# A gated state-space and linear-attention kernel: from a hand-written issue order to a list scheduler at trace time

## The chip, the cores and the metric

The kernel runs on one core of a Trainium2 chip. The metric is the device time of one execution in microseconds (us). Times are medians over all executions of a run. An execution is marked "slow" when it is over 1.5% above the fastest of the same kernel; ratios leave such executions out. A profile is one execution, so its span can differ by a microsecond or two from the median.

Engine names: PE is TensorE (matmuls; PEld is its weight load), DVE is VectorE, ACT is ScalarE, POOL is GpSimd, SP is SyncE, which issues the DMAs. The engines run side by side; in this program each takes its own instructions in the order in which they were issued, and waits on semaphores for the others. SBUF is the memory that the engines work in, PSUM the one into which PE writes its results; copying a result from PSUM to SBUF is called its evacuation. A fold multiplies a weight matrix with another one once, before the work on the rows. The tail is the time from PE's last matmul to the end.

## The reference, cut to what matters

The input is a sequence x of 2048 rows and 512 columns. Two branches are computed from it and mixed row by row by a sigmoid gate.

```python
x = A_x                                              # (1, 2048, 512)
g = _sigmoid((x * gate_w).sum(-1, keepdims=True))
# branch a: a diagonal complex recurrence over the rows
Bu = jnp.einsum("bld,pd->blp", x + 0j, B_bar)
for t in range(L):
    h = Lam_bar[None, :] * h + Bu[:, t, :]
y = 2.0 * jnp.einsum("blp,dp->bld", hseq, Cmat).real + x * Dskip
# branch b: linear attention, 32 heads of 16, softmax features of both signs
phi_k = concat([_softmax(pk), _softmax(-pk)])        # phi_q in the same way
kv  = jnp.einsum("bhsf,bhsd->bhfd", phi_k, v)
num = jnp.einsum("bhqf,bhfd->bhqd", phi_q, kv)
o = num / den                                        # ..., then @ wo
return g * a + (1 - g) * b
```

Both kernels check their own numbers and take a slower general path if a flag says that the fast one is not safe. The branch over that path is the last thing that every engine executes. With these inputs it is never taken.

## The kernel before

The order of issue is the order of the text. The author interleaved the units by hand:

```python
k_unit(0)                      # keys of 2 row tiles: features and the kv sum
g_unit(0)                      # inputs of the recurrence, block j = 0
for ti in range(8, 12):
    v_unit(ti)
k_unit(1)
k_unit(2)
scan_unit(0)                   # the recurrence and its three "fills"
g_unit(1)
# ... (cut) the same for j = 1, 2, 3; then kv is masked into KVbd and SM,
# ... then q features, then "mixing": 16 row tiles to the output
```

PSUM results have slots by purpose (two for keys, two for the kv sum, four for everything else):

```python
T_PK, T_KV, T_FILL = ("t0", "t1"), ("t2", "t3"), ("t4", "t5", "t6", "t7")
```

A key unit sums exponentials in a tree, lets POOL add the sums to a running check value, and divides by a reciprocal on DVE:

```python
        nc.gpsimd.tensor_tensor(out=smax[:], in0=smax[:], in1=cur..., op=ALU.add)
        rc = wk.tile([P, 32, 1, 4], BF16, name="rc", bufs=2)
        with nc.allow_low_precision("features are bf16"):
            nc.vector.reciprocal(out=rc[:], in_=cur)
        VT(out=E5, in0=E5, in1=rc[:].to_broadcast([P, 32, Dh, 4]), op=ALU.mult)
        # ... (cut) 16 matmuls add E to the kv sum
```

All three fills of a recurrence follow it at once:

```python
        cmul_add(Hs[:, j, 1, ...], z_prev, Gs[:, 1], ...)
        cmul_add(Hs[:, j, 0, ...], z_prev, Gs[:, 0], ...)
        cmul_add(Hs[:, j, 2, ...], Hs[:, j, 1, ...], Gs[:, 2], ...)
```

The fallback flag is computed after the third of four groups of mixing, so it is there well before the end.

## Time and profile before

| | before |
|---|---|
| time, median | 205.77 us (205.48 to 206.39, 3 runs) |
| span of the profiled run | 204.8 us |
| PE / DVE / ACT / POOL busy | 82% / 69% / 52% / 13% |
| chain of waits | PE 41%, DVE 41% |
| first PE instruction | 7.4 us |

Lines of the page of the kernel before: the span, each engine's busy time with its share and number of instructions, PE's busy tenths and its granted clock in 40 equal slices, and the engines' shares of the chain that ended last.

```profile
span 204.8 us, 3409 instructions
...
PE 167.7 (82%) x1310; PEld 92.4 (45%) x1330; DVE 142.2 (69%) x338; ACT 105.7 (52%) x190; POOL 27.4 (13%) x45
...
PE   0593299989997998489999990698999999999980
...
PEclk9999559999999999799999997579999999999999
...
PE 41%; DVE 41%; ACT 7%; DMA 4%; issue 3%; another core or an unknown queue 1%; ACTq 0%
```

PE is the busiest engine, but the chain is on DVE as often as on PE. The windows view of the kernel before tells the stages apart; the columns are the stretch, its length, and the busy time (and count) of PE, PEld, DVE, ACT and POOL, then the granted clock, the DMA share and GB/s.

```profile
...
core 0: us, PE busy (x) PEld busy (x) DVE busy (x) ACT busy (x) POOL busy (x), PEclk, DMA share, GB/s
...
10.00:26.00 16.00, 8.76 (x59) 4.72 (x58) 15.54 (x74) 10.47 (x16) 13.56 (x15) 0.80 0.89 229
...
50.00:110.00 60.00, 53.82 (x395) 27.29 (x400) 58.61 (x114) 33.39 (x62) 3.66 (x7) 0.97 0.00 1
...
122.00:130.00 8.00, 1.38 (x13) 0.56 (x12) 7.62 (x19) 3.66 (x8) 0.00 (x0) 0.72 0.00 0
130.00:170.00 40.00, 38.39 (x373) 23.04 (x376) 20.82 (x41) 19.30 (x38) 0.00 (x0) 0.93 0.08 25
```

From 50 to 110 us DVE has 1.4 us of slack in 60. From 122 to 130 us PE does almost nothing, and its granted clock falls (0.72 of full in this stretch, 0.93 in the next). The timeline of the kernel before shows what ends that gap (start, length, engine, line, operation, output<-inputs, and in brackets the idle time before it):

```profile
...
128.32 0.43 DVE L494 TENSOR_TENSOR KVbd<-kvacc_563,mask_78 64x256 bf16<-64x256 f32 x1
128.78 0.70 DVE L397 TENSOR_TENSOR Hs<-cm_1370,cm_1371 128x1024 bf16<-128x1024 bf16 x1
129.51 0.18 DVE L496 TENSOR_TENSOR SM<-kvacc_563,mask_78 64x16 bf16<-64x16 f32 x1
...
129.83 1.00 PE L530 MATMUL sm<-SM,ET 128*128 128x16 bf16 x32 [6.62 <-DVE SM L496]
```

PE waits 6.62 us for four small operations on SM, which stand in DVE's queue between the fills (Hs). The list of instructions on the running check value shows the POOL addition as a short operation (eight of them, 0.45 to 0.77 us); two of the eight are printed here. The three numbers are minimum, median and maximum in ns:

```profile
...
L445 POOL TENSOR_TENSOR smax<-smax,st_918 x1: 506/506/506, 80.9 to 80.9; 128x128 f32<-128x128 f32 x1
...
L445 POOL TENSOR_TENSOR smax<-smax,st_1328 x1: 456/456/456, 100.6 to 100.6; 128x128 f32<-128x128 f32 x1
```

Nothing waited for it: it was off the chain.

A sum over the weight-load records of the trace (one per matmul) gives PE's useful work at full clock: 154.7 us, if a matmul of N columns takes N/2.4 + 2.5 ns and at least 25 ns. These are the pitches of the trace, 0.216 us for 512 columns, 0.056 for 128, 0.025 for 16. Whatever else passes between the first and the last useful matmul is called PE's loss below. For the kernel before, it is 37.6 us.

### The profile page before, as it was taken

The numbers are of one execution on the slowest core, as the hardware profiler recorded it, in microseconds if no ns is written. First come the engines' busy times: TensorE is split into PE (matmuls) and PEld (weight loads), VectorE is DVE, ScalarE is ACT, GpSimd is POOL, SyncE is SP. The second block draws the span as 40 slices with busy tenths as digits, with TensorE's granted clock in tenths as the row PEclk, the third lists the DMA queues.
The fourth block names the chain that finished last, engine by engine and source line by source line (L and its number), as shares of the span: only waits on it lengthen the run. The fifth ranks groups of instructions, "written<-read, shape, count | busy, mean of one in ns | idle before, by whom it ended". The sixth has DMA issues, their size and how long they took to land.

```text
span 204.8 us, 3409 instructions
## 1 busy us (share of the span) xinstructions
PE 167.7 (82%) x1310; PEld 92.4 (45%) x1330; DVE 142.2 (69%) x338; ACT 105.7 (52%) x190; POOL 27.4 (13%) x45
## 2 busy tenths in 40 slices
PE   0593299989997998489999990698999999999980
PEld 0442148544443443274544440466545555555540
DVE  4199924562999999999999999859515339345330
ACT  2287387944782486455443895126475244333231
POOL 3459992000001000001200000000000000000000
PEclk9999559999999999799999997579999999999999
DMA  6999300000000000000000000000110100110101
GB/s 211 325 398 218 83 3 0 5 0 0 0 0 3 0 0 0 2 3 0 3 0 0 0 0 0 3 0 5 51 51 3 52 26 29 35 41 30 48 30 38
DMA packets 10991, 8.70 MB, mean 42 GB/s; under 512 B 5336, under 2 KB 10456, under 8 KB 10968
## 3 DMA queue, kind: packets, MB, share of 16 engines
q1 hardware_dynamic: 10928, 8.41, 14.0%
q8 instruction: 12, 0.20, 0.4%
q14 instruction: 11, 0.09, 0.2%
q10 hardware_dynamic: 40, 0.01, 0.0%
HBM read 5.26 MB, written 2.10 MB: 36 GB/s over the span
## 4 chain that ended last, share of the span: by engine, by line
PE 41%; DVE 41%; ACT 7%; DMA 4%; issue 3%; another core or an unknown queue 1%; ACTq 0%
PE py L563 13%; PE py L577 6%; DVE w L414 5%; PE pu L368 4%; DVE Hs L397 3%; DMA Wc<-in_B_w_phi_dram 3%; ACT oT L575 3%; PE pv L317 2%; DVE E L450 2%; DVE rc L448 2%; ACT E L166 2%; PE pu L371 2%; PE pt L573 2%; PE py L565 2%; DMA xn_101<-in_A_x_dram 2%
## 5 line engine op out<-in xcount | busy, mean ns | idle before, releaser
L563 PE MATMUL py<-CT,Hs 128*128 128x512 bf16 x127 | 33.7, 395 | 0.2
L387 ACT CAST Gs<-pu 128x512 bf16<-128x512 f32 x32 | 18.7, 588 | 23.2 <-PE pu L371 18.7
L368 PE MATMUL pu<-xT,BT 128*128 128x512 bf16 x124 | 29.7, 379 | 0.4 <-ACT Wq_66 L206 0.3
L166 ACT ACTIVATE E<-pk 128x512 bf16<-128x512 f32 x32 | 16.5, 601 | 7.3 <-PE kvacc_563 L454 5.7
L290 POOL TENSOR_SCALAR dgL<-ident,sp 128x128 bf16<-128x128 bf16 x24 | 19.3, 824 | 2.4 <-DVE sp L244 2.4
L368 PEld LDWEIGHTS <-BT 128*128 128x128 bf16 x128 | 12.4, 98 | 14.8 <-issue 0.5
L563 PEld LDWEIGHTS <-Hs 128*128 128x128 bf16 x128 | 12.7, 101 | 13.5 <-issue 1.9
L579 ACT ACTIVATE ot<-py,Gg 128x512 bf16<-128x512 f32 x16 | 11.0, 686 | 14.2 <-PE py L577 13.0
L434 PE MATMUL pk<-Wk_67,xT 128*128 128x512 bf16 x62 | 16.2, 391 | 2.0 <-ACT E L166 1.6
L317 PE MATMUL pv<-Wv,xT 128*128 128x512 bf16 x61 | 17.3, 441 | 0.4 <-issue 0.2
L575 ACT COPY oT<-pt 128x512 bf16<-128x512 bf16 x16 | 9.3, 584 | 16.0 <-PE pt L573 16.0
L577 PE MATMUL py<-Wo,oT 128*128 128x512 bf16 x56 | 14.8, 380 | 3.0 <-ACT oT L575 2.2
L371 PE MATMUL pu<-Gs,dgL 128*128 128x512 bf16 x48 | 13.1, 379 | 0.1
L166 ACT ACTIVATE ET<-pq 128x512 bf16<-128x512 f32 x24 | 11.9, 723 | 0.8 <-PE pq L463 0.8
L317 PEld LDWEIGHTS <-xT 128*128 128x128 bf16 x64 | 7.1, 112 | 10.0 <-issue 4.3
L318 ACT CAST vx<-pv 128x512 bf16<-128x512 f32 x16 | 9.3, 589 | 3.9 <-PE pv L317 3.8
L558 PE MATMUL pn<-KVbd,ET 128*128 128x128 bf16 x128 | 11.0, 226 | 0.0
L463 PE MATMUL pq<-xT,Wq_66 128*128 128x512 bf16 x47 | 10.3, 379 | 0.1
L434 PEld LDWEIGHTS <-xT 128*128 128x128 bf16 x64 | 6.2, 100 | 8.8 <-issue 3.4
L450 DVE TENSOR_TENSOR E<-E,rc 128x2048 bf16<-128x2048 bf16 x8 | 9.7, 1216 | 0.0
L577 PEld LDWEIGHTS <-oT 128*128 128x128 bf16 x64 | 5.0, 97 | 10.0 <-ACT oT L575 6.3
L530 PE MATMUL sm<-SM,ET 128*128 128x16 bf16 x128 | 4.1, 171 | 6.6 <-DVE SM L496 6.6
(319 smaller groups left out, 293.3 us busy)
## 6 DMA issues: line engine op xcount, KB each, us to landing
out_dram<-ot SPq DMA_DIRECT2D x16, 128.0 KB, 1.9
xn_101<-in_A_x_dram SPq DMA_DIRECT2D x1, 512.0 KB, 3.5
Wv<-in_B_wqkv_dram SPq DMA_DIRECT2D x1, 512.0 KB, 4.7
xn_102<-in_A_x_dram SPq DMA_DIRECT2D x1, 512.0 KB, 6.3
Wk_67<-in_B_wqkv_dram SPq DMA_DIRECT2D x1, 512.0 KB
Bn<-in_A_B_re_dram SPq DMA_DIRECT2D x1, 512.0 KB
Bn<-in_A_B_im_dram SPq DMA_DIRECT2D x1, 512.0 KB
xn_103<-in_A_x_dram SPq DMA_DIRECT2D x1, 512.0 KB
```

Source lines behind the costliest of these rows:

```text
L166: ins = nc.scalar.activation(**kw)
L290: nc.gpsimd.tensor_scalar(out=dgL[:, j, kk, :], in0=ident[:], scalar1=v[:, j:j + 1], scalar2=None, op0=ALU.mult)
L317: nc.tensor.matmul(out=pv[:], lhsT=xT[:, kt, tcols(f, a)], rhs=Wv[:, kt, :], start=(kt == 0), stop=(kt == KT - 1))
L368: nc.tensor.matmul(out=pu[:], lhsT=BT[:, ri, kt, js], rhs=xT[:, kt, f * NCH:(f + 1) * NCH], start=(kt == 0), stop=(kt == KT - 1 and not ex ...
L371: nc.tensor.matmul(out=pu[:], lhsT=dgL[:, j, kk, :], rhs=rhs, start=False, stop=(n == len(extra) - 1))
L387: nc.scalar.copy(out=Gs[:, f, ri, :], in_=pu[:])
L434: nc.tensor.matmul(out=pk[:], lhsT=xT[:, kt, tcols(f, a)], rhs=Wk2[:, kt, :], start=(kt == 0), stop=(kt == KT - 1))
L450: VT(out=E5, in0=E5, in1=rc[:].to_broadcast([P, 32, Dh, 4]), op=ALU.mult)
L558: nc.tensor.matmul(out=pn[:, sgn, g * P:(g + 1) * P], lhsT=ET[:, sgn, g, cs], rhs=KVbd[:, sgn, g, :], start=True, stop=True)
L563: nc.tensor.matmul(out=py[:], lhsT=Hs[:, j, f, ri, zs], rhs=CT[:, ri, j, :], start=(j == 0 and ri == 0), stop=False)
L575: nc.scalar.copy(out=oT[:], in_=pt[:])
L577: nc.tensor.matmul(out=py[:], lhsT=oT[:, g, :], rhs=Wo[:, g, :], start=False, stop=(g == HG - 1))
```

## The change

The intent: write the work as tasks with an engine (or a choice of engines), a duration, dependencies, buffers and a rank; let a list scheduler place them at trace time; issue the instructions in the order that it found. PSUM slots are taken from any bank that is free. Nine dummy matmuls run while the first block of x is loaded. The diff has 1,307 lines; this is its core.

```diff
+class _Plan:
+    def add(self, eng, fn, deps=(), follow=(), bufs=(), rank=0.0): ...
+    def run(self):
+        # (cut) for each engine: among the tasks that can start within 40 ns of
+        # the earliest, the highest rank first, then the order of the text
+                r, took, t = min((w for w in rs if w[0] <= t0 + 40.0), key=lambda w: (-w[2].rank, w[2].n))
+        self.order = sorted(out, key=lambda t: (t.start, t.n))
+
+def _pe(n, cols):
+    return {"PE": n * max(30.0, cols / 2.4 + 3.0)}
+def _dve(*elems):
+    return {"DVE": sum(e / 0.96 + 70.0 for e in elems)}
+def _act(*elems):
+    return {"ACT": sum(e / 1.2 + 100.0 for e in elems)}
...
+    pl.pool("A", 4, psum("a"))
+    pl.pool("B", 2, psum("b"))
+    pl.pool("C", 2, psum("c"))
+    A1 = ("A", "B")
+    d_vec, d_wc = pl.at(5.5), pl.at(6.0)          # when loads are believed to land
+    def warm_fn(e):
+        for _ in range(NWARM):                    # NWARM = 9
+            MM(out=bw.t[:], lhsT=warm[:, 0:P], rhs=warm[:], start=True, stop=True)
...
         # in a key unit
-        nc.gpsimd.tensor_tensor(out=smax[:], in0=smax[:], in1=cur..., op=ALU.add)
-            nc.vector.reciprocal(out=rc[:], in_=cur)
+        t_sx.append(pl.add({"POOL": 450.0}, lambda e: nc.gpsimd.tensor_tensor(
+            out=smax[:], in0=smax[:], in1=b1.t..., op=ALU.add), deps=prev + t_sx[-1:], bufs=[b1]))
+        x = pl.add(_act(128), lambda e: aact(out=b1.t[:], in_=b1.t[:], func=ACT.Ln), deps=prev + t_sx[-1:], ...)
+        x = pl.add(_act(128), lambda e: aact(out=rc.t[:], in_=b1.t[:], func=ACT.Exp, scale=-1.0), deps=[x], ...)
...
+    for f in (0, 2):                              # eight of the twelve fills
+        for j in range(PT):
+            fill_unit(j, f, -1)                   # lowest rank
...
+    x = pl.add({"DVE": 600.0}, fl1, deps=t_qm + [t_fk, t_tn])   # the flag: rank 0, last in the text
```

Smaller edits: one of three sine tables is dropped, evacuations of PSUM go to ACT or DVE, and the masking of kv has rank 5.

## The prediction

> **What bounds the kernel now.** The page gives PE 82% busy, DVE 69%; the chain of waits is shared, PE 41%, DVE 41%. The windows view splits the 204.8 us:
> - 0 to 7.5 us: PE idle. The first x block landed at 4.2 us (chain), but PE's first instruction, the small vector transpose, waits for five short DMAs until 7.4.
> - 7.5 to 16: the v matmuls run cold, 0.43 us each, against 0.216 later (four in 0.86, chain).
> - 16 to 27: PE busy 3.7 of 11 us; the fold waits 4.2 us for one evacuation behind the sine tables on DVE.
> - 50 to 129: DVE busy 77.2 of 79 us, PE 67.0.
> - 122.7 to 129.8: PE waits 6.6 us for the masked state, whose operations stand in DVE's queue behind the last recurrence; the granted clock then falls to 0.71.
> - 153 to 200: mixing, 3.73 us a tile.
> - 200 to 204.8: last output.
>
> **PE's floor.** 560 matmuls of 512 columns at 0.216 us are 121 us; 448 of 128 columns at 0.057 (eight in 0.46) 25.5; kv, sums and gate columns some 10 (25 to 45 ns each). Estimate: 157 us at full clock. The other 48 us are idle time and half clock.
>
> **What the change does.** Nine dummy matmuls (0.43 us cold, 3.9 us) run before x lands; the Trainium skill, "TensorE: Matmul & The Clock Gate", section "What's actually happening", says a busy window of about 3.4 us releases the clock. Here it became full only after some microseconds of work, so this should save about 3 us. Not waiting for the vectors saves another 2 to 3.
> In the DVE-bound stretch: eight reciprocals (0.945 us, 7.6 in all) become Ln and Exp on ACT (0.3 to 0.4 each, estimated from 0.40 for 128x128); eight of the twelve recurrence fills (2.36 us each, 19 us) get low rank and can run in the mixing stage, where DVE is half idle; evacuations go to whichever engine is free. DVE's demand there falls by some 25 us, below PE's (about 70), so PE becomes the limit. The kv extraction gets a high rank, and q matmuls can fill its wait: 6.6 us and 2 to 3 of slow clock go. One sine table of three is dropped (2.1 us ACT). ACT gains 5 to 6 us and some evacuations; DVE plus ACT, about 245 us of 2x175, fit. Two 512-wide scalings (about 0.69 each) replace one of 1.22: harmless. In mixing I expect 3.73 to near 3.51 per tile, as other work fills the wait for the transposed copy.
>
> **Sum.** PE useful work from about 5 us, plus 157, plus 4.8 us of tail makes 167. I add 4 us for early stalls (loads until 15 us, table loads, crowded ACT), 4 for waits where the fixed order meets durations other than assumed (0.53 us for a 512 ACT copy; the trace has 0.59), and 1 from span to time: 176 us, about 14% less.
>
> **To check.** First useful PE work near 5 us, clock full; DVE below 90% and PE nearly solid from 50 to 129; no gap of several us around the masked state; the chain goes to PE (over 70%); reciprocals gone; a tail of 5 us.
>
> **What would make it wrong.** In-order queues: one late producer blocks an engine's head and the delay spreads; ACT crowded in the first 30 us; PSUM slots held by accumulating tiles; a longer tail because low-rank fills push the last tiles; PE at reduced clock under denser load. Then 180 to 190. Less waiting than I allow: 169.
>
> Chances: faster by over 2%: 0.95; within 2%: 0.04; slower: 0.01. Range 169 to 184.

## The result, and the profile after

| | before | after |
|---|---|---|
| time, median | 205.88 us (205.48 to 206.39, 4 runs) | 186.08 us (185.27 to 187.28, 4 runs) |
| ratio | | 0.9042, 95% interval 0.8981 to 0.9103 |
| span of the profiled run | 204.8 us | 183.5 us |
| first useful weight load on PE | 7.4 us | 4.6 us |
| useful work on PE, full clock | 154.7 us | 154.7 us |
| PE's loss between first and last useful matmul | 37.6 us | 16.7 us |
| from PE's last matmul slot to the end | 5.1 us | 7.5 us |

The last four rows of a column add up to its span. A ratio here and below is the mean time of one kernel's fast runs over that of the other's of the same rounds, so it is not quite the ratio of the medians.

The change made the kernel 9.6% faster. It was forecast at 176 us, 14% faster, and the measured time lies outside the range of 169 to 184. So the question is where the last 10 us went. The same lines of the page, after:

```profile
span 183.5 us, 3424 instructions
...
PE 164.0 (89%) x1316; PEld 92.0 (50%) x1339; DVE 141.6 (77%) x338; ACT 98.0 (53%) x194; POOL 33.1 (18%) x48
...
PE   7987779999999999977996999899999999999930
...
PEclk9999799999999999999997899999999999999996
...
PE 45%; DVE 30%; SPq 8%; POOL 4%; DMA 4%; issue 3%; ACT 2%; ACTq 0%; POOLq 0%
```

PE is denser, but the chain is only 45% on PE, and 4% of it is on POOL, which was not on it at all. (The 8% on SPq, the queue from which SyncE issues DMAs, is an early stretch of DMA issues that the control's profile of the same kernel doesn't have on its chain: there PE has 51%, DVE 31%, POOL 4%. So only the share of POOL is read as a finding.) The same stretches after the change, with the columns as before:

```profile
...
10.00:26.00 16.00, 11.65 (x94) 7.43 (x95) 14.65 (x62) 14.36 (x25) 10.87 (x13) 0.89 0.98 230
...
50.00:110.00 60.00, 55.67 (x398) 27.34 (x404) 54.21 (x110) 35.95 (x74) 8.75 (x5) 0.97 0.00 1
...
122.00:130.00 8.00, 7.95 (x75) 5.22 (x76) 8.00 (x18) 4.77 (x10) 0.00 (x0) 1.00 0.14 49
130.00:170.00 40.00, 39.63 (x326) 23.40 (x332) 28.14 (x59) 15.18 (x29) 0.00 (x0) 1.00 0.10 34
```

The gap from 122 to 130 us is gone, and the mixing (130 to 170) is solid on PE at full clock. From 50 to 110 us DVE is no longer full (54.21 of 60), yet PE still is not either (55.67). From 10 to 26 us PE is busy 11.65 of 16, with DVE and ACT both close to full.

The masking of kv, after, in the timeline:

```profile
...
107.96 0.43 DVE L772 TENSOR_TENSOR KVbd<-pp,mask_80 64x256 bf16<-64x256 f32 x1
...
108.18 1.17 PE L843 MATMUL pp<-SM,ET 128*128 128x16 bf16 x31
108.31 0.17 DVE L774 TENSOR_TENSOR SM<-pp,mask_80 64x16 bf16<-64x16 f32 x1
108.51 0.69 DVE L645 TENSOR_TENSOR c<-c,Tcs 128x1024 bf16<-128x1024 bf16 x1
```

PE's sums (L843) now follow the masking closely, and the recurrence's next step (L645) stands behind it instead of before it. That much is as forecast.

The new wait shows in the instructions on the check value, after. The last two lines are from the list of those who waited for it (us, times):

```profile
...
L714 POOL TENSOR_TENSOR smax<-smax,st_747 x1: 457/457/457, 43.9 to 43.9; 128x128 f32<-128x128 f32 x1
...
L714 POOL TENSOR_TENSOR smax<-smax,st_1066 x1: 1978/1978/1978, 75.9 to 75.9; 128x128 f32<-128x128 f32 x1
L714 POOL TENSOR_TENSOR smax<-smax,st_1131 x1: 2647/2647/2647, 82.2 to 82.2; 128x128 f32<-128x128 f32 x1
...
  ACT st_1249 L239: 2.8, 1
  ACT st_1131 L239: 2.4, 1
```

An addition that took 0.45 to 0.77 us takes up to 2.65, and ACT waits for it. Ln overwrites the sum in place, so it cannot start before POOL has read it. The timeline after shows one such place:

```profile
...
75.64 0.69 DVE L669 TENSOR_TENSOR c<-c 128x1024 bf16<-128x1024 bf16 x1
...
75.87 1.98 POOL L714 TENSOR_TENSOR smax<-smax,st_1066 128x128 f32<-128x128 f32 x1 [13.91 <-DVE st_1066 L711]
...
76.24 0.69 DVE L711 TENSOR_TENSOR st_1078<-E 128x1024 bf16<-128x1024 bf16 x1
...
76.84 0.69 DVE L672 TENSOR_TENSOR Hs<-c,Hs 128x1024 bf16<-128x1024 bf16 x1
...
77.88 0.31 ACT L239 ACTIVATE st_1066<-st_1066 128x128 f32<-128x128 f32 x1 [1.39 <-POOL smax L714]
...
78.22 0.31 ACT L239 ACTIVATE rc<-st_1066 128x128 bf16<-128x128 f32 x1
...
78.56 1.22 DVE L718 TENSOR_TENSOR E<-E,rc 128x2048 bf16<-128x2048 bf16 x1 [1.03 <-ACT rc L239]
...
79.85 0.33 PE L725 MATMUL pp<-vx,E 128*128 128x68 bf16 x5 [0.96 <-DVE E L718]
```

POOL's addition starts at 75.87 us and ends at 77.85, 0.3 us after the last of three DVE operations with two SBUF inputs. Ln on ACT starts at once, then Exp, then the product on DVE, and PE's kv matmuls (L725) 4.0 us after POOL started. The Trainium skill, "SBUF — State Buffer", section "Who interferes with whom", states that a VectorE instruction with two SBUF inputs contends with a GpSimd instruction that reads SBUF, and that the one that comes later is blocked. This trace agrees: 0.46 us at 34.0 and 37.1 us, where DVE is idle, 1.98 and 2.65 us beside such instructions.

The swap did two things at once. In the kernel before, DVE went on to the reciprocal, which has one input, soon after each sum was ready (at 80.89 us POOL starts, at 81.00 the reciprocal). With the reciprocal gone, operations with two inputs follow at once. This is read from the two traces; no run separates it from the waiting of Ln.

At the end of the trace there are records that the views do not count as busy. These are the branch records over the fallback, in plain output (start in us, length in ns, engine; Tensor is PE, and GpSimd's is left out):

```
before  196.94    72 Vector   199.61  3981 Tensor   200.63    50 Scalar   201.19    45 Sync
after   177.98    72 Vector   177.82  4621 Tensor   177.75    50 Scalar   178.13    45 Sync
```

Before, PE reads the flag and branches while the last output is still being scaled and stored. After, the flag is the last task of all: DVE writes it at 177.18 us, 1.2 us after PE's last matmul slot, and only then do all engines read it. PE's branch then takes 4.6 us with nothing left to hide it.

### The profile page after: what moved, and what is told of

The parts are those of the page before. It is cut to its first block, busy times and chain, and to the rows that moved or that the text cites. A ratio compares the mean times of both kernels' runs of the same rounds, so it can differ in the third digit from the quotient of the medians.

```text
span 183.5 us, 3424 instructions
## 1 busy us (share of the span) xinstructions
PE 164.0 (89%) x1316; PEld 92.0 (50%) x1339; DVE 141.6 (77%) x338; ACT 98.0 (53%) x194; POOL 33.1 (18%) x48
## 4 chain that ended last, share of the span: by engine, by line
PE 45%; DVE 30%; SPq 8%; POOL 4%; DMA 4%; issue 3%; ACT 2%; ACTq 0%; POOLq 0%
PE pp L896 14%; PE pp L913 7%; SPq L314 6%; DVE c L642 5%; POOL smax L714 4%; PE pp L883 4%; PE pp L595 4%; DVE E L718 3%; PE pp L694 3%; DMA vec_n<-in_A_log_dt_dram 2%; PE pp L907 2%; PE pp L403 2%; PE pp L788 2%; PE pp L900 2%; DVE c L664 2%
## 5 line engine op out<-in xcount | busy, mean ns | idle before, releaser
L896 PE MATMUL pp<-CT,Hs 128*128 128x512 bf16 x124 | 30.8, 379 | 0.2
L595 PE MATMUL pp<-xT,BT 128*128 128x512 bf16 x123 | 30.0, 379 | 0.2
L362 ACT CAST Hs<-pp 128x512 bf16<-128x512 f32 x26 | 14.9, 604 | 10.3 <-PE pp L608 4.7
L239 ACT ACTIVATE E<-pp 128x512 bf16<-128x512 f32 x32 | 16.6, 613 | 1.1 <-PE pp L694 1.1
L239 ACT ACTIVATE ET<-pp 128x512 bf16<-128x512 f32 x32 | 16.3, 624 | 0.2 <-PE pp L788 0.2
L913 PE MATMUL pp<-Wo,oT 128*128 128x512 bf16 x59 | 15.7, 379 | 0.3
L788 PE MATMUL pp<-xT,Wq_68 128*128 128x512 bf16 x61 | 15.3, 402 | 0.4 <-issue 0.2
L403 PE MATMUL pp<-Wv,xT 128*128 128x512 bf16 x61 | 15.5, 395 | 0.1
L694 PE MATMUL pp<-Wk_69,xT 128*128 128x512 bf16 x62 | 14.7, 379 | 0.1
L909 ACT COPY oT<-pp 128x512 bf16<-128x512 bf16 x16 | 9.3, 582 | 9.3 <-PE pp L913 5.6
```

What stands on the lines that cost most here:

```text
L239: return nc.scalar.activation(**kw)
L362: nc.scalar.copy(out=out_ap, in_=view(b))
L403: MM(out=f32v(b), lhsT=xT[:, kt, tcols(f, a)], rhs=Wv[:, kt, :], start=(kt == 0), stop=(kt == KT - 1))
L595: MM(out=f32v(b), lhsT=BT[:, ri, kt, js], rhs=xT[:, kt, f * NCH:(f + 1) * NCH], start=(kt == 0), stop=(kt == KT - 1 and f % 2 == 0))
L694: MM(out=f32v(b), lhsT=xT[:, kt, tcols(f, a)], rhs=Wk2[:, kt, :], start=(kt == 0), stop=(kt == KT - 1))
L788: MM(out=f32v(b), lhsT=Wq2[:, kt, g * P:(g + 1) * P], rhs=xT[:, kt, f * NCH:(f + 1) * NCH], start=(kt == 0), stop=(kt == KT - 1))
```

## The experiments

Each is an edit of the changed kernel unless another base is named. Losses and tails are sums over the profiled run as in the table above. Runs of one call share a chip and the runs of the kernel before. The control belongs to the first call (control, the first two mends, the early flag); runs of the other two calls are safer to compare by their ratios.

In all of these runs but the control and the one without dummies, the scheduler placed the tasks anew, so an edit also moves work that it does not name: with Ln in its own tile about 12% of PE's weight loads stand at another place in the order. A single gain can be partly luck of a new order; a cause is called shown here where the trace shows the wait and more than one edit that removes it gains.

### Control

```diff
 (no edit)
```

> The changed kernel again, unedited, as the control of this call. Both theories: 186 us (185.3 to 187.3 in the four runs so far), span about 184, PE's last useful matmul about 176 us, the sums of GpSimd in the key stage 1.4 to 2.6 us long when they meet VectorE additions.

Measured: 186.34 us (184.84 to 186.74), ratio 0.9027 (0.8997 to 0.9057). PE's loss 16.7 us, 7.7 of them between 60 and 122 us, tail 6.9 us. It repeats.

### Ln into its own tile

```diff
+    sb("ln", 2, [P, 32, 1, 4], F32)
-        x = pl.add(_act(128), lambda e: aact(out=b1.t[:], in_=b1.t[:], func=ACT.Ln), deps=prev + t_sx[-1:], bufs=[b1], ...)
-        x = pl.add(_act(128), lambda e: aact(out=rc.t[:], in_=b1.t[:], func=ACT.Exp, scale=-1.0), deps=[x], bufs=[b1, rc], ...)
+        ln = pl.buf("ln")
+        x = pl.add(_act(128), lambda e: aact(out=ln.t[:], in_=b1.t[:], func=ACT.Ln), deps=prev, bufs=[b1, ln], ...)
+        x = pl.add(_act(128), lambda e: aact(out=rc.t[:], in_=ln.t[:], func=ACT.Exp, scale=-1.0), deps=[x], bufs=[ln, rc], ...)
```

> Ln writes to its own tile instead of over the sum that GpSimd still has to read, so nothing waits for GpSimd. Theory A (the late part of the loss comes from the GpSimd addition, which the change put on the chain between the feature sums and the kv matmuls; 3 kv waits of 1.3, 1.4 and 1.8 us on PE): those waits shrink below 0.5 us each, 4 to 5 us are gained: 181.5 us. Rival B (the plan just does not fit the real durations of VectorE and ScalarE, and the addition only happens to stand beside the waits): less than 1.5 us gained.

Measured: 181.55 us (180.21 to 182.35), ratio 0.8798 (0.8762 to 0.8835), 4.8 us less than the control. PE's loss between 60 and 122 us fell from 7.7 to 3.5 us. Theory A holds. One wait of 1.04 us stayed (before the kv matmuls at about 99 us), so the forecast of "below 0.5 each" was missed there. The POOL addition itself became no shorter, only unimportant; its records in this run (minimum, median, maximum in ns):

```profile
...
L715 POOL TENSOR_TENSOR smax<-smax,st x8: 454/668/4852, 34.0 to 96.3; 128x128 f32<-128x128 f32 x8
```

One of the eight took 4.85 us, and nobody cared.

### The addition on DVE

```diff
-        t_sx.append(pl.add({"POOL": 450.0}, lambda e: nc.gpsimd.tensor_tensor(
+        t_sx.append(pl.add(_dve(128), lambda e: VT(
```

> The same addition on VectorE instead of GpSimd (0.2 to 0.3 us each), Ln still waits for it. Theory A in its narrow form (it is the length of the GpSimd operation, held up by VectorE's two-input operations, not the dependency): nearly as much gained as with the separate tile, 3.5 to 4.5 us, 182 us. If the dependency itself costs: only about half of that. Rival B: nothing, or 2 us slower for 8 more operations on VectorE.

Measured: 180.05 us (179.04 to 180.46), ratio 0.8711 (0.8681 to 0.8741), 6.3 us less than the control. The dependency of Ln on the addition is still there; only the engine changed:

```profile
...
L714 DVE TENSOR_TENSOR smax<-smax,st x8: 269/286/293, 34.5 to 99.7; 128x128 f32<-128x128 f32 x8
```

So most of the cost was the length of the POOL operation beside DVE's traffic, not the dependency, and rival B falls: eight more DVE operations made the kernel faster. It also beat the separate tile by 1.5 us, which the theory did not say. Part of it is in PE's loss from 60 to 122 us (2.9 against 3.5); the rest is left open.

### The flag earlier

```diff
-    x = pl.add({"DVE": 600.0}, fl1, deps=t_qm + [t_fk, t_tn])
+    x = pl.add({"DVE": 600.0}, fl1, deps=t_qm + [t_fk, t_tn], rank=4)
 (rank=4 also on the transpose and on the last step of the flag)
```

> The flag of the fallback branch gets rank 4, so it is computed some 10 us before the end instead of last. Theory: each engine reads the flag and branches after its own last work; in the changed kernel all five wait for the flag at 177.2 us, 1.3 us after PE's last matmul, and PE's branch then takes 4.6 us. With the flag early PE branches at once: the tail from PE's last matmul to the end falls from 7.5 to about 6 us; 1.3 us gained in all, 184.8 us. Rival: the tail is the last output's transfer; then nothing is gained.

Measured: 184.25 us (183.16 to 184.28), ratio 0.8925 (0.8899 to 0.8952), 2.1 us less than the control. The tail fell to 5.6 us in the kept profile, near the 5.1 us of the kernel before; PE's loss did not change (16.8). The branch on PE starts at 173.67 us in this run and takes 3.3 us, beside the last matmuls and the start of the last scaling; it is over before the last store is issued (177.25).

### No dummy matmuls

```diff
-        for _ in range(NWARM):
+        for _ in range(0):
```

> The changed kernel with none of the nine dummy matmuls sent, the order of everything else as planned with them. The prediction's theory: PE runs its first 3 to 4 us of real work at half clock, so 2 to 3 us slower (188 to 189 us). Rival: between 10 and 26 us PE waits for VectorE and ScalarE anyway (6 us lost there in the changed kernel), so a slow start is absorbed there: less than 1 us slower.

Measured: 187.22 us (184.56 to 187.88) over six executions. Three of them (187.46 to 187.88) count as slow, so the ratio, 0.8989 (0.8933 to 0.9046), rests on the other three (184.56, 184.72 and 186.98). Against the control's 0.9027 it shows no loss; the intervals overlap. It was run at another time. With the slow ones the mean is 186.5 us, against 186.0 for the control, so a loss of up to about a microsecond cannot be excluded. The prediction's 2 to 3 us for the warm start are not there, and the rival fits the times. Its mechanism, that the early waits absorb the slow start, is not shown, because the profiled run of this kernel fell in the slow state and is not compared.

### All fills at once

```diff
-    fill_unit(0, 1)
+    for f_ in (1, 0, 2):
+        fill_unit(0, f_)
 (the same for j = 1, 2, 3; the eight fills of rank -1 removed)
```

> All twelve recurrence fills stand right after their recurrence at rank 0, none is deferred to the mixing stage. Theory: VectorE is then again the limit of the key stage, and about 3 to 5 us come back: 189 to 191 us, VectorE over 95% busy from 50 to 110 us. Rival: the key stage is held up by the GpSimd addition and not by VectorE's load: less than 1.5 us slower.

Measured: 188.23 us (187.28 to 189.0), ratio 0.9128 (0.909 to 0.9166): 1.9 us more than the control's median, between theory and rival. DVE is full again in the key stage, at 57.43 of 60 us:

```profile
...
50.00:110.00 60.00, 56.88 (x352) 26.73 (x356) 57.43 (x114) 37.62 (x77) 5.43 (x4) 0.98 0.00 1
```

The loss came back where the kernel before had its gap: 4.3 us between 122 and 130 us, where the changed kernel has none. Deferring the fills is real, but about half of what was expected. The changed kernel also defers less than the text suggests: of its eight fills of lowest rank, the scheduler placed four so early that they ended before 130 us.

### Reciprocals back on DVE

```diff
-        (Ln and Exp on ACT)
+        def rcp(e):
+            with nc.allow_low_precision("features are bf16"):
+                nc.vector.reciprocal(out=rc.t[:], in_=b1.t[:])
+        x = pl.add({"DVE": 860.0}, rcp, deps=prev, bufs=[b1, rc], rank=rank + 1)
```

> The eight reciprocals go back to VectorE (about 0.95 us each) in place of Ln and Exp on ScalarE; nothing waits for the GpSimd addition then. Theory: Ln over the sum's tile is what put GpSimd on the chain; without it 4 to 5 us are gained, 7 us of VectorE work cost 2 to 3 of it: 183 to 185 us, faster than the changed kernel, so the swap in the form in which it was made was a loss. The prediction's theory (the swap unloads VectorE and is a gain): 188 us or more.

Measured: 182.67 us (181.72 to 183.52), ratio 0.886 (0.8824 to 0.8897). Undoing this part of the change made it 3.7 us faster. So the swap, as made, was a loss, and it is the part that put POOL on the chain. With the separate tile the swap may be a small gain after all: 0.8798 against 0.886, and the intervals just overlap.

### PSUM slots by purpose again

```diff
-    A1 = ("A", "B")
+    A1 = ("A",)                                   # keys and gate: "B"
-    A2, A3 = ("A", "C"), ("B", "C")
+    A2, A3 = ("C",), ("B",)
-        pn = [pl.buf(*A2), pl.buf(*A2)]
+        pn = [pl.buf("A"), pl.buf("A")]
```

> PSUM slots divided by purpose as in the kernel before (four for general use, two for keys, two for kv; in mixing four for the kv products, two for outputs, two for the rest), the scheduler run again under that limit. Theory: any-bank slots are worth something while six results wait for evacuation, mostly in the first 30 us: 1.5 to 3 us slower, 188 to 189 us. Rival: banks are not scarce: within 0.8 us.

Measured: 188.49 us (188.28 to 190.16), ratio 0.9164 (0.9123 to 0.9205): 2.2 us more than the control's median. PE's loss rose by 3.2 us to 19.9, about 1.1 of it before 30 us and the rest between 60 and 130 us. The size was as expected, the place only in half.

### Both mends

```diff
 (the addition on DVE, and the flag at rank 4)
```

> Both mends at once: the addition on VectorE, the flag at rank 4. If the two losses are separate (one in the key stage, one in the tail) the gains add: 180.1 minus 2.1, about 178 us. If they overlap: 179 or more.

Measured: 178.36 us (176.75 to 179.11), ratio 0.8626 (0.8584 to 0.8669). The gains add.

### Both mends, and what the scheduler believes of the start

```diff
-    d_vec, d_wc = pl.at(5.5), pl.at(6.0)
+    d_vec, d_wc = pl.at(7.2), pl.at(7.2)
-    fq_, _ = fold(Wq2, d_wq, fk_pf)
+    fq_, _ = fold(Wq2, d_wq, fk_pf, -3)           # ranks 3 and 4 become 0 and 1
```

> As the run with both mends, and two edits of what the scheduler believes: the small vectors arrive at 7.2 us instead of 5.5 (PE waited 0.7 to 1.8 us for them with its third or fourth task), and the q weights are folded at rank 0 instead of 3, so that they do not go ahead of the v and x work. The plan that the scheduler prints has 3.1 us of PE idle time between 5 and 26 us instead of 6.1. Theory (the early loss is mostly in the plan itself): 2 to 3 us faster, about 175.5 us. Rival (early, durations are off so far that the plan means little): less than 1 us.

Measured: 177.22 us (175.94 to 177.46), ratio 0.8582 (0.8549 to 0.8616). PE's loss before 30 us fell from 9.5 to 6.2 us in the profiled runs, as forecast, but the median gained only 1.1 us, and the two intervals overlap. The mechanism shows; the gain is at the edge of what these rounds resolve. This is the fastest correct kernel with its fallback in place. Its page:

```profile
span 175.0 us, 3407 instructions
...
PE 163.3 (93%) x1317; PEld 91.1 (52%) x1339; DVE 140.7 (80%) x343; ACT 99.0 (57%) x197; POOL 23.3 (13%) x40
...
PE   7997699999999999999999999889999999999970
...
PE 52%; DVE 37%; DMA 3%; ACT 2%; issue 2%; ACTq 1%; DVEq 0%
```

### Without most of the table work (wrong result)

```diff
-                VS(out=psi[:, j], in0=iot[:], ...)
+                VS(out=psi[:, j, 0:8], in0=iot[:, 0:8], ...)
 (8 of 512 columns in every step of the sine tables, the rest a constant; base: both mends)
```

> WRONG RESULT on purpose. As the run with both mends, but the sine tables are computed over 8 columns instead of 512 (the rest of the table is a constant), which takes some 8 us of VectorE and 4 us of ScalarE work out of the first 26 us. Theory (PE's 6 us of loss there are waits for evacuations by the two crowded engines): the loss falls to 2 us and the time by about 4: 174 us. Rival (the loads come too late for PE, or the cold clock costs it): no change.

Measured: 174.95 us (173.96 to 175.61), ratio 0.8467 (0.8434 to 0.8499), 3.4 us less than its base; the result is wrong. PE is busy 14.22 us of the stretch from 10 to 26, against 11.65 in the changed kernel and 11.93 in the base:

```profile
...
10.00:26.00 16.00, 14.22 (x152) 10.05 (x153) 13.65 (x75) 15.00 (x32) 11.13 (x20) 1.00 0.97 230
```

The loads and the dummies are the same, so the early loss is for the most part a wait for the evacuating engines, not for data. PE's loss before 30 us fell from 9.5 to 4.5 us. A part of it is clock: in the base the granted clock is at half for 3.4 us from 20.8 us on (0.89 of full over the stretch), here it stays full (1.00). By the doubled pitches that is worth at most 1.7 us (an estimate).

### Without the branch

```diff
-    with tc.If(flag_i != 0):
-        general_path(...)
-    return nc.values_load(flag_i[0:1, 0:1], min_val=0, max_val=1)
+    return None
 (base: both mends)
```

> As the run with both mends, but without the branch to the fallback and without the fallback's code (the results are the same for these inputs). Theory: of the 5.5 us from PE's last matmul to the end some 1 to 2 us are the branch on PE (3.3 to 4.6 us of record): 176 to 177 us. Rival: the tail is the last output's transfer and the closing of the queues: no change.

Measured: 176.45 us (175.98 to 177.58), ratio 0.8565 (0.8529 to 0.8601), 1.9 us less than its base. The tail fell from 5.6 to 3.9 us. But these 1.7 us are not PE's branch, as the theory had it: in the base it ends at 172.86 us, before the last store is issued at 172.87, 1.2 us after PE's last matmul slot in both runs. What differs comes later. The store takes 3.0 us from issue to landing in the base and 1.9 without the branch, and from landing to the end it is 1.4 us against 0.8. In the base three blocks of instructions (32 KB) are fetched from 173.6 to 175.1 us, beside the store; without the branch none is fetched after 156.7. That these fetches delay the store is likely, and not shown by itself.

## Why the prediction was wrong

The direction and the main mechanisms held. The sum was 10 us too low because three of its terms were too small: the early stalls, the later waits and the tail. Each term of the sum, as the prediction put it, beside the trace of the profiled run:

| term | forecast | measured |
|---|---|---|
| first useful PE work | about 5 | 4.6 |
| useful work | 157 | 154.7 |
| early stalls | 4 | 8.9 (loss before 30 us) |
| later waits | 4 | 7.8 (16.7 minus 8.9) |
| tail | 4.8 | 7.5 |
| from span to time | 1 | 1.8, and 0.8 more to the median |

1. **Early stalls, 4.9 us too small.** The prediction named "crowded ACT" as a risk and gave all early stalls 4 us. Before the change ACT and DVE together were busy 26.0 of the 32 engine-microseconds from 10 to 26 us; after it 29.0, with PE asking for evacuations faster. The timeline after shows PE's transposes (L549) held at 18.02 and 19.54 us until ACT has freed PSUM:

```profile
...
12.37 2.04 ACT L362 COPY WT<-pp 128x512 bf16<-128x512 bf16 x4
...
18.02 0.38 PE L549 MATMUL pp<-ident,Wq_68 128*128 128x128 bf16 x4 [1.28 <-ACT Wk_69 L362]
...
18.92 1.06 ACT L362 CAST Wk_69<-pp 128x512 bf16<-128x512 f32 x2
...
19.54 1.56 PE L549 MATMUL pp<-ident,Wq_68 128*128 128x128 bf16 x12 [1.14 <-ACT Wk_69 L362]
```

   Taking the table work away removed 5.0 us of this loss (on the base with both mends, and with the clock's part in it). It was also foreseeable in the change itself: the schedule that its own scheduler makes, with its own assumed durations, already has 6.1 us of PE idle time between 5 and 26 us and practically none later.

2. **Later waits, 3.8 us too small, and for another reason than given.** The step that failed is "eight reciprocals become Ln and Exp on ACT", costed only as DVE time saved. The edit also made Ln overwrite a tile that POOL reads, and so put a POOL addition on the chain. Its plan gives that addition 0.45 us; beside DVE it took up to 2.65. Two separate mends removed 4.8 and 6.3 us, and undoing the swap removed 3.7. The reason given, that a 512-column ACT copy takes 0.59 us where the plan has 0.53, was a misreading. 0.59 is the length of a record. Four copies in a row take 2.04 us in the lines above, and their records start 0.48 us apart, so the plan's figure was not too short. The Trainium skill, "ScalarE: Activation LUTs", section "What ACT_TABLE_LOAD costs", says that back-to-back ACTIVATEs overlap by about 93 ns; the records of these copies overlap by 0.11 to 0.14 us.

3. **Tail, 2.7 us too small.** The prediction carried over 4.8 us from the kernel before without asking what was hidden in it. The flag had been early; the scheduler, with rank 0 and the last place in the text, put it at the very end. Moving it brought back 2.1 us.

4. **The warm start, only half there, and no gain seen.** The prediction expected a full clock at the first useful work. In the profile after it was not full (the PEclk row of the page shows 9 there, but the record of the clock only begins at 6.6 us):

```profile
...
1.18 4.02 PE L379 MATMUL pp<-warm 128*128 128x512 bf16 x9 [1.18 <-DVE warm L298]
...
4.99 1.48 PE L390 MATMUL pp<-ident,xn 128*128 128x128 bf16 x12
...
8.92 1.06 PE L390 MATMUL pp<-ident,xn 128*128 128x128 bf16 x16
```

   The first transposes of x start 0.107 us apart, later ones 0.056. Full clock was granted at 6.6 us, 5.4 us after the first dummy; in the control, the same kernel, at 4.2. The Trainium skill, "TensorE: Matmul & The Clock Gate", section "What's actually happening", gives about 3.4 us of sustained work and says that the window runs free of the kernel's start; nine dummies, 3.9 us in all, are barely one such window. In the kernel before the clock was full only at 12.9 us, so the dummies did bring it forward. But taking them away cost nothing that the fast executions show. The start at 4.6 instead of 7.4 us came from no longer waiting for the small vectors at the head of PE.

5. **What held.** The gap around the masked state went (7.0 us of loss before, none after), and so did the loss in mixing (7.4 us of loss after 130 us before, 0.4 after). The fills were worth about 2 us and the free choice of banks about 2 us. Of the checks, DVE "below 90%" from 50 to 129 us failed narrowly: 54.21 of 60 up to 110, then full up to 130. The step "DVE's demand there falls by some 25 us" was mis-sized: of the 79 us from 50 to 129 DVE was busy 73.2 in the changed kernel and 77.2 in the kernel before. Other work was drawn into the room: 13 of the 32 products of the mixing stage (L887) ran before 130 us, and only four of the eight deferred fills ended after it. Evacuations are not the reason: DVE has one (L364) after 50 us. The chain did not go to PE (45%, 51% in the control, not 70%); with the mends it is 52%.

How much the new order is worth by itself was not tried alone: no kernel here has the tasks without the scheduler. That it closed the gap of the masked state and filled the mixing is read from the two traces.

## What to carry to other kernels

When an operation moves to another engine, look at what it now has to wait for: writing in place over a tile that a slow, unimportant reader still needs makes that reader important. A list scheduler is only as good as its weakest duration, and a duration that depends on what a neighbouring engine does at that moment is the weakest kind; keep such operations off the chain instead of tuning their number. Give work that ends the program, such as a flag for a branch, a rank, since nothing else in a schedule tells it that everyone waits for it. And a low rank is no promise that a task comes late: it fills whatever room is free, here before 130 us for four of eight fills.

## What the Trainium skill lacked or had wrong

- "SBUF — State Buffer", "Who interferes with whom", has the rule that explains the POOL addition, and the traces agree. It does not say how long a GpSimd operation can be held by a stream of VectorE instructions: here 0.46 us became 1.98, 2.65 and once 4.85 us, and the one of 2.65 us (82.20 to 84.85) runs across five VectorE instructions, not one.
- "Advanced Engine Details and Errata", "Control Flow Timing", gives about 108 ns for a compare-and-branch. Here the record is 45 to 72 ns on the other engines, and 3.3 to 4.6 us on PE over the fallback. "Runtime: NRT & Kernel Launch", "Instruction fetch mechanics", does warn that a taken branch out of the prefetched window waits for a DMA fetch, but has no size for it. The traces agree in part: in the changed kernel blocks of 8 and 16 KB of instructions are fetched from 178.7 to 182.5 us, while PE's branch lasts from 177.8 to 182.4; without the branch none is fetched at the end, and the tail is 1.7 us shorter. That the branch waits for a fetch is not shown by itself.
- "TensorE: Matmul & The Clock Gate", section "What's actually happening", says that the point of transition varies by 500 ns either way. In the twelve profiled runs here with nine dummies, which all start at 1.2 us, full clock was granted 3.0 to 6.0 us after the first of them. The page also puts the cost of the ramp below 1% of a typical kernel; the ratio of 0.8989 without the dummies, against 0.9027 with them, does not contradict that.
